# Chunk attention and ELU feed-forward: w_in operands kept by column tile, w_out's raw high quarters written later, out writes scheduled one by one

## The chip, the cores and the metric

The kernel runs on one core of a Trainium2 chip. The metric is the device time of one execution in microseconds (us), read as a median over runs. TensorE (PE) multiplies, VectorE (DVE), ScalarE (ACT) and GpSimd (POOL) work on tiles, and SyncE (SP) issues nearly all DMAs, in program order, from one queue.

## The reference

Eight heads of 576 tokens in 8 batches are attended in chunks of 64 tokens; the heads of a token are then laid side by side (4608 tokens of 512) and go through a feed-forward net with an ELU between its two products.

```python
scores = scale * np.matmul(q_c, k_c.transpose(0, 1, 2, 4, 3))   # 64 x 64 in each chunk
scores = scores - np.max(scores, axis=-1, keepdims=True)
attn = np.exp(scores)
attn = attn / (np.sum(attn, axis=-1, keepdims=True) + 1e-09)
out = np.matmul(attn, v_c)
...
h = x @ w_in                                                     # 4608 x 512 by 512 x 2048
g = np.where(h > 0.0, h, alpha * (np.exp(np.minimum(h, 0.0)) - 1.0))
return (g @ w_out).astype(np.float32)                            # by 2048 x 512
```

## The kernel before

**Precision.** Each operand of the feed-forward net is kept as a high part of fewer bits and a low part (names ending in `hi` and `lo`), and a product is three matmuls of 128x128 by 128x512 (`three`, line 431; its matmul is line 434). The weights arrive as 64-bit floats and are rebuilt from their halves in `prepare_units` and `merge_units`.

**Stages.** The 4608 tokens are 9 blocks of 512. Three are computed plainly: the first (with the loading of the weights among it), the second and the third (`FIRST_BLOCK`, `SECOND_BLOCK`/`LATER`, `THIRD_BLOCK`: strings in which each item is one step, emitted in that order). The other six are taken in three pairs, and each pair multiplies by a scheme of seven products of quarter matrices instead of eight, for w_in and again for w_out. The first pair is written out by hand (`PAIR`, and `KEPT` for its w_out products). The other two, called superblocks here, are ordered by a planner.

**Operands of the seven products.** For w_in they are made during the second block by `combine` (line 512): POOL adds and subtracts quarters (line 510), `write_parts` (line 534) writes the raw quarters from `wi_hi` and `wi_lo` to `a_dram` (line 537), `write_sums` (line 547) the four sums. For w_out, `Sums` makes four sums for each of eight pairs of row tiles j (`whole`, line 576; `sum`, line 591; `high`, 594; `low`, 597; `write_half`, 603) and writes them to `w_dram`; `write_raw` (line 652) writes raw quarters, two DMAs a call. In the superblocks the operands come back as entries of 512 KB into a ring of four slots (`load_entry`, line 1317). The low parts of w_out are also kept in `lo_dram` and loaded again into `wo_lo` (line 689).

**Attention.** While a block is multiplied, the attention of coming tokens runs beside it in tiles of 128 tokens: loads of q and k (line 227) and of v (line 206), turns by DVE (line 351), scores (line 248), softmax, a turn of the result by DVE (line 388), a copy by ACT (line 393), a swap of quarters between partitions by four small DMAs on SP's queue (`swap_turned`, line 399), and the product with v (`multiply_v`, line 256), which waits for that swap.

**Who sets the order.** The engines run their instructions in the order of the program. Up to `KEPT` that is the order of the strings; what `MORE_KEPT` and `RAW_SECOND` name is spread among their lines. In the superblocks the class `Plan` sets it: each job has a nominal time, estimated costs, what it reads and writes, and a due time followed back from the PE products that need it. A job of SP may hold several DMAs, and these are then issued as one. `add_sums` (line 1873) adds the w_out sums that are left (j of 2, 6 and 7, `LATE_SUMS`), `add_out` (line 1630) the writes of finished results: two turns by DVE (line 1637), then four DMAs (line 1645). `add_entry` adds the ring loads.

**Places.** The sums of j = 6 and 7 use room of the tiles `g_more`, in which the superblocks later keep hidden values (`g_place`); `g_more` lies in the places of `wo_hi` and `wo_lo` of the first half of w_out, and row 4 to 7 of it is named by `g`.

Of the kernel before, what the change touches and what calls it, by code (L numbers as in the profile page):

```python
# [10 lines left out]
F32 = mybir.dt.float32  # L11
F32R = mybir.dt.float32r
# [8 lines left out]
def kernel(  # L21
# [34 lines left out]
    Q = 32  # L56
# [32 lines left out]
    def w_in_tiles(pool):  # L89
        return [pool.tile([P, NK, NF // 2 * P], F32R, name=name) for name in ("wi_hi", "wi_lo")]  # L90
# [4 lines left out]
    def w_in_slices(f: int):  # L95
        half, f = divmod(f, NF // 2)
        return [w[:, :, f * P:(f + 1) * P] for w in weights[half][:2]]
# [414 lines left out]
    def combine():  # L512
# [18 lines left out]
        def rows(i: int, g: int, lo: int):  # L531
            return a_dram[i, g // 2, :, g % 2, lo].rearrange("p (k f) -> p k f", k=2)

        def write_parts(g, lo):
            w1, w2 = w_in_slices(2 * g)[lo], w_in_slices(2 * g + 1)[lo]
            for i, w in enumerate((w1[:, :2], w1[:, 2:], w2[:, 2:])):
                nc.sync.dma_start(out=rows(i, g, lo), in_=w.bitcast(F32))
# [454 lines left out]
    def dma(n: int, took: float):  # L992
        return 540 * n, 540 * (n - 1) + 2000 + took, took
# [24 lines left out]
    def warm(n: int):  # L1018
# [83 lines left out]
    RAW_SECOND = {3: (3, 1), 6: (4, 1), 9: (5, 1), 13: (3, 0), 14: (4, 0), 15: (5, 0)}  # L1102
# [11 lines left out]
        2: "w1a w1b", 3: "w1c", 4: "w1d", 5: "w1e w1f", 6: "w1g", 7: "w1h", 8: "w1i", 9: "w1j", 11: "R0", 13: "R1",  # L1114
        14: "R2", 15: "R3",
# [265 lines left out]
    def g_place(j: int, b: int):  # L1381
        if j < 4:
            return g_first[:, j, b]
        name = ("wo_hi", "wo_lo")[j // 2 - 2]
        return late_tile(name, lambda: w0.tile([P, 2, 4, TB], F32, name="g_more", tag=name))[:, j % 2, b]
# [46 lines left out]
    LATE_SUMS = (2, 0), (6, 6), (7, 18)  # L1432
# [197 lines left out]
    def add_out(t: float, s: int, h: int, c: int, sources, keys, place, place_keys):  # L1630
# [11 lines left out]
        def send():  # L1642
            for b in range(4):
                at = b * P + c * 2 * Q
                nc.sync.dma_start(
                    out=out[n0:n0 + TB, at:at + 2 * Q].rearrange("(t p) d -> p t d", p=Q),
                    in_=place()[b * Q:(b + 1) * Q].rearrange("p (t d) -> p t d", d=2 * Q))
# [3 lines left out]
        plan.add(t + .05, "SP", dma(4, 2300), send, list(place_keys), [])  # L1651
# [221 lines left out]
    def add_sums(t: float, j: int):  # L1873
        made, early = {}, j < NG // 2
        g = 2 if early else 4 + j % 2
# [9 lines left out]
        def whole(engine):  # L1885
# [6 lines left out]
            ("G", i, b) for i in ((4, 5) if early else (6, 7)) for b in range(4)]  # L1892
# [52 lines left out]
```

## Time and profile before

| what | value |
|---|---|
| median of 3 runs | 836.18 us (833.5 to 837.43) |
| the profiled execution | 833.86 us, of it 832.1 us span |
| mean granted PE clock | 0.992 |
| PE busy | 810.0 us (97%) |
| DVE, ACT, POOL busy | 616.4, 524.7, 171.5 us |
| moved by DMA | 191.90 MB, mean 231 GB/s |
| first, second, third block about | 27 to 130, 130 to 235, 235 to 325 us |
| hand-written pair, `KEPT`, superblocks about | 325 to 454, 454 to 505, 505 to 832 us |

In the profile a row of a group has the line, the engine, the operation and output<-inputs. `SPq` is SP issuing a DMA; the time beside it is that of the issue, not of the transfer. A row of a timeline has start, duration, engine, line, what, and in brackets how long the engine stood idle before it and what ended that. A row of a stretch has the stretch, its length, then the busy time of PE, PE's weight loads, DVE, ACT and POOL with instruction counts, the granted PE clock, the mean busy share of the 16 DMA engines, and GB/s.

### The profile page before, as it was taken

To read this page: it belongs to the slowest core of one execution; us is meant where nothing else is said; L and a number is where in the kernel's file an instruction comes from. 1 tells how busy PE (TensorE), PEld (TensorE's weight loads), DVE (VectorE), ACT (ScalarE), POOL (GpSimd) and SP (SyncE) were. 2 spreads that over 40 slices of the span, in tenths; PEclk is the share of its full clock that TensorE was granted. 3 is DMA by queue.
4 is the path that set the end of the run, shared out by engine and by line. 5 is a ranking of instruction groups with operands and counts; after the bars stand their busy time and mean duration, and the time that the engine had idled before them with its cause. 6 is when DMAs were issued, how large, how long until landed. Compare 5 with 4: busy or idle time off the path is not lost.

```text
span 832.1 us, 15856 instructions
## 1 busy us (share of the span) xinstructions
PE 810.0 (97%) x5853; PEld 659.8 (79%) x5853; DVE 616.4 (74%) x915; ACT 524.7 (63%) x990; POOL 171.5 (21%) x148
## 2 busy tenths in 40 slices
PE   7899999999989999999999999999999999999997
PEld 6688878888768878878888888877788878888886
DVE  4999997676856668767666867877799956557974
ACT  5999885444554545766666445988867736776551
POOL 0000014365425441434111263100020000000100
PEclk9999999999999999999999999999999999999999
DMA  9875984888879797679977787999865586555655
GB/s 259 249 223 192 298 289 132 246 258 243 251 222 248 208 264 213 215 242 268 291 228 193 213 235 247 317 272 274 253 203 205 189 245 204 187 194 201 212 194 152
DMA packets 189629, 191.90 MB, mean 231 GB/s; under 512 B 84976, under 2 KB 158192, under 8 KB 189552
## 3 DMA queue, kind: packets, MB, share of 16 engines
q1 hardware_dynamic: 188912, 188.80, 75.9%
q0 software_dynamic: 640, 2.10, 0.6%
q8 instruction: 46, 0.75, 0.4%
q14 instruction: 31, 0.25, 0.1%
HBM read 144.18 MB, written 42.99 MB: 225 GB/s over the span
## 4 chain that ended last, share of the span: by engine, by line
PE 78%; DMA 9%; DVE 4%; ACT 4%; SPq 3%; issue 1%; DVEq 0%; ACTq 0%
PE o L434 41%; PE h L434 32%; DMA ring<-a_dram 3%; PE ps_a L248 2%; PE ps_a L256 2%; DMA kept<-in_k_dram 1%; DMA turned<-unturned 1%; DMA kept<-in_q_dram 1%; SPq L227 1%; PE h L451 1%; SPq L206 1%; SPq L399 1%; PE ps_a L315 1%; DMA k_sb<-in_k_dram 1%; DMA wo_lo<-lo_dram 1%
## 5 line engine op out<-in xcount | busy, mean ns | idle before, releaser
L434 PE MATMUL o<-wo_hi,ghi 128*128 128x512 f32 x272 | 108.3, 398 | 0.0
L434 PE MATMUL o<-wo_hi,glo 128*128 128x512 f32 x272 | 107.0, 393 | 0.5 <-DVE glo L479 0.5
L434 PE MATMUL o<-wo_lo,ghi 128*128 128x512 f32 x272 | 106.6, 392 | 0.0
L434 PE MATMUL h<-xhi,wi_hi 128*128 128x512 f32 x228 | 83.9, 397 | 0.1
L434 PE MATMUL h<-xlo,wi_hi 128*128 128x512 f32 x228 | 82.3, 390 | 0.0
L434 PE MATMUL h<-xhi,wi_lo 128*128 128x512 f32 x180 | 70.2, 390 | 0.0
L434 PEld LDWEIGHTS o<-wo_hi,glo 128*128 128x128 f32 x272 | 51.3, 189 | 12.3 <-DVE glo L479 1.4
L434 PEld LDWEIGHTS o<-wo_hi,ghi 128*128 128x128 f32 x272 | 51.5, 189 | 11.3
L434 PEld LDWEIGHTS o<-wo_lo,ghi 128*128 128x128 f32 x272 | 51.5, 189 | 10.4
L510 POOL TENSOR_TENSOR kept<-wi_hi,wi_lo 128x512 f32<-128x512 f32 x16 | 22.2, 1405 | 157.9 <-DVE xf L172 117.8
L471 DVE SCALAR_TENSOR_TENSOR e<-e,h 128x512 f32<-128x512 f32 x48 | 32.8, 684 | 25.0 <-ACT e L469 24.7
L434 PE MATMUL o<-split,ring 128*128 128x512 f32 x216 | 51.0, 390 | 0.0
L434 PEld LDWEIGHTS h<-xhi,wi_hi 128*128 128x128 f32 x228 | 42.6, 188 | 9.8 <-ACT kept L785 0.8
L434 PEld LDWEIGHTS h<-xlo,wi_hi 128*128 128x128 f32 x228 | 42.8, 188 | 8.6
L434 PEld LDWEIGHTS o<-split,ring 128*128 128x128 f32 x216 | 40.5, 188 | 8.4
L393 ACT COPY unturned<-turned 128x512 f32<-128x512 f32 x28 | 17.4, 621 | 46.0 <-DVE turned L388 40.1
L468 ACT ACTIVATE e<-h 128x512 f32<-128x512 f32 x48 | 28.6, 597 | 27.5 <-PE h L434 21.9
L476 ACT CAST ghi<-e 128x512 fp32r<-128x512 f32 x48 | 29.8, 621 | 20.3 <-DVE e L471 20.2
L746 POOL TENSOR_TENSOR glo<-e,ghi 128x512 fp32r<-128x512 f32 x16 | 20.8, 1297 | 96.8 <-ACT ghi L744 96.8
L434 PE MATMUL h<-split,ring 128*128 128x512 f32 x168 | 40.4, 392 | 0.0
L1492 ACT ACTIVATE e<-e 128x512 f32<-128x512 f32 x64 | 39.5, 630 | 1.0
L434 PEld LDWEIGHTS h<-xhi,wi_lo 128*128 128x128 f32 x180 | 33.8, 188 | 7.2
(226 smaller groups left out, 2021.4 us busy)
## 6 DMA issues: line engine op xcount, KB each, us to landing
ring<-a_dram SPq DMA_DIRECT2D x56, 512.0 KB, 4.7
ring<-w_dram SPq DMA_DIRECT2D x56, 512.0 KB, 3.3
wi_hi<-a_dram SPq DMA_DIRECT2D x56, 256.0 KB, 5.1
kept<-in_q_dram SPq DMA_DIRECT2D x100, 128.0 KB, 3.4
kept<-in_k_dram SPq DMA_DIRECT2D x100, 128.0 KB, 4.0
wo_lo<-lo_dram SPq DMA_DIRECT2D x20, 512.0 KB, 5.7
v_sb<-in_v_dram SPq DMA_DIRECT2D x32, 256.0 KB, 5.6
st<-in_moe_w_in_dram SPq DMA_DIRECT2D x16, 512.0 KB, 4.2
```

What stands on the lines that cost most here:

```text
L206: nc.sync.dma_start(out=dst[p0:p0 + n], in_=src[b, :, s0:s0 + n, :].rearrange("h s d -> s h d"))
L227: nc.sync.dma_start(out=qk[p0:p0 + n // U, w0:w0 + NK * U * D].rearrange("p (h w) -> p h w", h=NK), in_=src[b, j::2, s0:s0 + n, :].rearran ...
L248: nc.tensor.matmul(scores[halves[c], j, hp, :], lhsT=qT[halves[j], hp, halves[c]], rhs=kT[halves[j], hp, halves[c]], start=True, stop=True,)
L256: nc.tensor.matmul(x_ps[halves[j], c, hp, :], lhsT=v_sb[halves[c], 2 * hp + j, :], rhs=aT[halves[c], :, j * NK + hp], start=True, stop=True,)
L393: nc.scalar.copy(out=unturned, in_=turned)
L434: nc.tensor.matmul(ps, lhsT=a, rhs=b, start=start, stop=stop, skip_group_check=onto)
L468: nc.scalar.activation(out=e, in_=h, func=AF.Relu, scale=-1.0)
L471: nc.vector.scalar_tensor_tensor(out=e, in0=e, scalar=-1.0, in1=h, op0=ALU.add, op1=ALU.max)
L476: nc.scalar.copy(out=ghi, in_=e)
L510: nc.gpsimd.tensor_tensor(out=out, in0=a, in1=b, op=op)
L746: engine.tensor_tensor(out=lo, in0=e, in1=hi.bitcast(F32), op=ALU.subtract)
L1492: nc.scalar.activation(out=units[u], in_=units[u], func=AF.Exp, scale=-1.0)
```

## The change

Four things change; what is computed stays.

1. `wi_hi` and `wi_lo` hold, for each tile of 128 columns, its four row tiles side by side (before: for each row tile all columns). A quarter that `write_parts` writes is then 1 KB in a row of SBUF instead of two runs of 512 B, and two of the three writes become one DMA: two DMAs a call instead of three.
2. The raw high quarters of the second half of w_out (`write_raw(3..5, 0)`, six DMAs of 256 KB) leave the second block (f = 13, 14, 15) for `KEPT` (f = 8, 10, 12).
3. The four DMAs of `add_out` become four jobs of the planner.
4. The sums of j = 6 and 7 have later nominal times (8 and 22 products after the start of the first superblock instead of 6 and 18) and rows 6 and 7 of `g_more` as their room instead of 4 and 5; rows 4 and 5 now lie where `wo_lo` was.

```diff
-        return [pool.tile([P, NK, NF // 2 * P], F32R, name=name) for name in ("wi_hi", "wi_lo")]
+        return [pool.tile([P, NF // 2, NK * P], F32R, name=name) for name in ("wi_hi", "wi_lo")]
...
-        return [w[:, :, f * P:(f + 1) * P] for w in weights[half][:2]]
+        return [w[:, f].rearrange("p (k f) -> p k f", k=NK) for w in weights[half][:2]]
...
-        def rows(i: int, g: int, lo: int):
-            return a_dram[i, g // 2, :, g % 2, lo].rearrange("p (k f) -> p k f", k=2)
-
         def write_parts(g, lo):
             w1, w2 = w_in_slices(2 * g)[lo], w_in_slices(2 * g + 1)[lo]
-            for i, w in enumerate((w1[:, :2], w1[:, 2:], w2[:, 2:])):
-                nc.sync.dma_start(out=rows(i, g, lo), in_=w.bitcast(F32))
+            nc.sync.dma_start(
+                out=a_dram[:2, g // 2, :, g % 2, lo, :].rearrange("i p w -> p i w"),
+                in_=w1.rearrange("p (i k) f -> p i (k f)", k=2).bitcast(F32))
+            nc.sync.dma_start(
+                out=a_dram[2, g // 2, :, g % 2, lo, :], in_=w2[:, 2:].rearrange("p k f -> p (k f)").bitcast(F32))
...
-    RAW_SECOND = {3: (3, 1), 6: (4, 1), 9: (5, 1), 13: (3, 0), 14: (4, 0), 15: (5, 0)}
+    RAW_SECOND = {3: (3, 1), 6: (4, 1), 9: (5, 1)}
...
-        2: "w1a w1b", 3: "w1c", 4: "w1d", 5: "w1e w1f", 6: "w1g", 7: "w1h", 8: "w1i", 9: "w1j", 11: "R0", 13: "R1",
-        14: "R2", 15: "R3",
+        2: "w1a w1b", 3: "w1c", 4: "w1d", 5: "w1e w1f", 6: "w1g", 7: "w1h", 8: "w1i W3", 9: "w1j", 10: "W4", 11: "R0",
+        12: "W5", 13: "R1", 14: "R2", 15: "R3",
...
-        name = ("wo_hi", "wo_lo")[j // 2 - 2]
+        name = ("wo_lo", "wo_hi")[j // 2 - 2]
...
-    LATE_SUMS = (2, 0), (6, 6), (7, 18)
+    LATE_SUMS = (2, 0), (6, 8), (7, 22)
...
-        def send():
-            for b in range(4):
-                at = b * P + c * 2 * Q
-                nc.sync.dma_start(
-                    out=out[n0:n0 + TB, at:at + 2 * Q].rearrange("(t p) d -> p t d", p=Q),
-                    in_=place()[b * Q:(b + 1) * Q].rearrange("p (t d) -> p t d", d=2 * Q))
+        def send(b: int):
+            at = b * P + c * 2 * Q
+            nc.sync.dma_start(
+                out=out[n0:n0 + TB, at:at + 2 * Q].rearrange("(t p) d -> p t d", p=Q),
+                in_=place()[b * Q:(b + 1) * Q].rearrange("p (t d) -> p t d", d=2 * Q))
...
-        plan.add(t + .05, "SP", dma(4, 2300), send, list(place_keys), [])
+        for b in range(4):
+            plan.add(t + .05 + .01 * b, "SP", dma(1, 575), lambda b=b: send(b), list(place_keys), [])
...
-        g = 2 if early else 4 + j % 2
+        g = 2 if early else 6 + j % 2
...
-            ("G", i, b) for i in ((4, 5) if early else (6, 7)) for b in range(4)]
+            ("G", i, b) for i in ((6, 7) if early else (4, 5)) for b in range(4)]
```

PE's order of products stays as it was; the tables of the change move SP's DMAs above all. Three places of SP's queue follow. A row is line, DMA, output<-input, shape, and how many in a row.

The end of the second block and the start of the third, before: the writes of w_in's quarters (`a_dram<-wi_..`), of sums (`a_dram<-kept`) and of w_out's raw high quarters (`w_dram<-wo_hi`) stand ahead of a swap of the attention (`turned<-unturned`).

```order
L537 DMA a_dram<-wi_lo 128x2x128 x3
L652 DMA w_dram<-wo_hi 256x1x256 x2
L547 DMA a_dram<-kept 128x4x256 x2
L537 DMA a_dram<-wi_hi 128x2x128 x3
L652 DMA w_dram<-wo_hi 256x1x256 x2
L537 DMA a_dram<-wi_lo 128x2x128 x3
L227 DMA kept<-in_q_dram 16x4x256 x8
L227 DMA kept<-in_k_dram 16x4x256 x8
L652 DMA w_dram<-wo_hi 256x1x256 x2
L547 DMA a_dram<-kept 128x4x256 x2
L537 DMA a_dram<-wi_hi 128x2x128 x3
L399 DMA turned<-unturned 32x256 x4
```

The same place in the change, from the second half of the first write on:

```order
L536 DMA a_dram<-wi_lo 128x256
L547 DMA a_dram<-kept 128x4x256 x2
L533 DMA a_dram<-wi_hi 128x2x256
L536 DMA a_dram<-wi_hi 128x256
L533 DMA a_dram<-wi_lo 128x2x256
L536 DMA a_dram<-wi_lo 128x256
L227 DMA kept<-in_q_dram 16x4x256 x8
L227 DMA kept<-in_k_dram 16x4x256 x8
L547 DMA a_dram<-kept 128x4x256 x2
L533 DMA a_dram<-wi_hi 128x2x256
L536 DMA a_dram<-wi_hi 128x256
L399 DMA turned<-unturned 32x256 x4
```

Ten DMAs fewer stand between the swap before this one and the swap shown: four of w_in's writes, six raw quarters. What follows the swap (loads of q, k and v, writes of the first block's results, the next swap) stays in its order.

The end of `KEPT`, before: sums of j = 1 (`w_dram<-g_kept`), loads for the attention, the first four ring entries, and the low parts of j = 2 (`g_kept<-lo_dram`).

```order
L603 DMA w_dram<-g_kept 128x2x256 x2
L689 DMA wo_lo<-lo_dram 128x1024
L227 DMA kept<-in_q_dram 32x4x256 x4
L227 DMA kept<-in_k_dram 32x4x256 x4
L1317 DMA ring<-a_dram 128x1024 x4
L584 DMA g_kept<-lo_dram 128x1024
```

The same place in the change:

```order
L603 DMA w_dram<-g_kept 128x2x256
L652 DMA w_dram<-wo_hi 256x1x256 x2
L603 DMA w_dram<-g_kept 128x2x256
L689 DMA wo_lo<-lo_dram 128x1024
L227 DMA kept<-in_q_dram 32x4x256 x4
L227 DMA kept<-in_k_dram 32x4x256 x4
L652 DMA w_dram<-wo_hi 256x1x256 x2
L1317 DMA ring<-a_dram 128x1024
L652 DMA w_dram<-wo_hi 256x1x256 x2
L1317 DMA ring<-a_dram 128x1024 x3
L584 DMA g_kept<-lo_dram 128x1024
```

The six raw quarters now stand ahead of the ring's entries 2 to 4 and of the low parts, four of them ahead of the first entry too.

The start of the last superblock, before: ring entries and out writes.

```order
L1317 DMA ring<-a_dram 128x1024 x2
L1645 DMA out_dram<-g_kept 32x16x64 x8
L1317 DMA ring<-a_dram 128x1024 x2
L1645 DMA out_dram<-g_kept 32x16x64 x4
L1317 DMA ring<-a_dram 128x1024 x24
```

In the change:

```order
L1317 DMA ring<-a_dram 128x1024 x2
L1644 DMA out_dram<-g_kept 32x16x64 x5
L1317 DMA ring<-a_dram 128x1024
L1644 DMA out_dram<-g_kept 32x16x64 x3
L1317 DMA ring<-a_dram 128x1024
L1644 DMA out_dram<-g_kept 32x16x64
L1317 DMA ring<-a_dram 128x1024
L1644 DMA out_dram<-g_kept 32x16x64 x3
L1317 DMA ring<-a_dram 128x1024 x23
```

The third ring entry has three out writes fewer ahead of it, the fifth three fewer; the fourth as many as before. In the first superblock the eight writes of the sums of j = 6 and 7 stand later among the ring loads (before, three of the eight stood ahead of the superblock's first swap, now none), three loads of q earlier, and of the work on these sums one addition moves from POOL to DVE and two subtractions from DVE to POOL.

## The prediction

> **What bounds the kernel now.** I read the page's busy times first, then the list of waits for PE alone, then the stretches in which PE is not full.
>
> ```profile
> PE 810.0 (97%) x5853; PEld 659.8 (79%) x5853; DVE 616.4 (74%) x915; ACT 524.7 (63%) x990; POOL 171.5 (21%) x148
> PE ps_a L256 <- DMA turned<-unturned: 2.9, 3, 2.4
> PE h L434 <- DMA ring<-a_dram: 1.8, 2, 1.3
> PE o L434 <- DMA ring<-a_dram: 1.3, 4, 0.7
> ```
>
> PE is the bound: 22 us of 832.1 are not busy, and PE's program stays as it is. The change can only give or take idle time of PE, and what a pause does to PE's clock. The waits say where: one of 2.4 us for a swap of the attention, and six for ring entries, 3.1 us together. The stretches around them (length, then PE, PE's loads, DVE, ACT, POOL; clock, DMA share and GB/s last):
>
> ```profile
> 244.00:250.00 6.00, 3.35 (x71) 2.48 (x70) 1.42 (x2) 1.81 (x3) 4.53 (x3) 0.94 0.72 201
> 248.00:254.00 6.00, 5.82 (x46) 4.73 (x47) 4.17 (x8) 1.73 (x3) 2.25 (x3) 0.72 0.74 214
> 540.00:544.00 4.00, 3.65 (x17) 2.69 (x16) 2.49 (x5) 3.84 (x12) 0.00 (x0) 1.00 1.05 361
> 560.00:572.00 12.00, 10.40 (x44) 7.68 (x43) 9.17 (x15) 9.32 (x17) 0.00 (x0) 1.00 1.01 271
> 584.00:592.00 8.00, 7.10 (x29) 5.15 (x29) 6.88 (x12) 7.73 (x15) 0.00 (x0) 1.00 0.95 250
> 676.00:686.00 10.00, 8.23 (x35) 6.24 (x35) 4.06 (x6) 5.70 (x10) 0.00 (x0) 1.00 1.03 293
> ```
>
> Row one: PE idles 6.00 - 3.35 = 2.65 us. Row two: behind that pause the clock is granted at 0.72 of full speed for 6 us, which costs (1 - 0.72) x 6 = 1.7 us more. No other pause after the first block costs clock: the rows from 540 on have 1.00. So there are three pools of time: **4.3 us** at the swap, 0.35 + 1.60 + 0.90 = **2.85 us** in the first superblock, and **1.77 us** at the start of the last one.
>
> **Quarters of w_in and w_out, second block.** The swap that PE waits for, with what SP issues ahead of it (SP's rows of the timeline, then ACT's copy that feeds the swap, and PE):
>
> ```profile
> 204.90 2.48 SPq L399 DMA_DIRECT2D turned<-unturned  x4
> ...
> 208.04 1.69 SPq L537 DMA_DIRECT2D a_dram<-wi_lo  x3
> 209.78 1.26 SPq L652 DMA_DIRECT2D w_dram<-wo_hi  x2
> ...
> 212.40 2.57 SPq L537 DMA_DIRECT2D a_dram<-wi_hi  x3
> 215.00 1.19 SPq L652 DMA_DIRECT2D w_dram<-wo_hi  x2
> 216.24 1.73 SPq L537 DMA_DIRECT2D a_dram<-wi_lo  x3
> ...
> 226.10 1.19 SPq L652 DMA_DIRECT2D w_dram<-wo_hi  x2
> ...
> 228.62 2.93 SPq L537 DMA_DIRECT2D a_dram<-wi_hi  x3
> ...
> 239.59 0.62 ACT L393 COPY unturned<-turned 128x512 f32<-128x512 f32 x1 [2.70 <-DVE turned L388]
> 243.68 3.12 SPq L399 DMA_DIRECT2D turned<-unturned  x4
> 247.65 0.30 PE L256 MATMUL ps_a<-turned,v_sb 64*64 64x64 f32 x2 [2.42 <-DMA turned<-unturned]
> ```
>
> From 204.90 SP issues without a pause: each row begins where the one ahead ends. ACT has the data ready at 239.59 + 0.62 = 240.21, SP comes to the swap at 243.68, 3.5 us late, and PE has stood since 247.65 - 2.42 = 245.23. The change takes out of that queue one of three issues at four places, (1.69 + 2.57 + 1.73 + 2.93) / 3 = 2.97 us, and six raw quarters, 1.26 + 1.19 + 1.19 = 3.64 us: 6.6 us. SP would be at the swap by 243.68 - 6.6 = 237.1, so the copy becomes the last to come, at 240.21. From issue to PE's start it took 247.65 - 243.68 = 3.97 us, with all its traffic beside it; the same again ends at 244.2, 1.0 us ahead of need. The stall goes with its clock: **-4.3 us**. Bounds: 0 if the transfer turns out to be what is late, -4.3 if all goes. I take the upper one, for the margins are 3.1 us on SP's queue and 1.0 us behind it. What is late next there: nothing by more than the other two waits of that row, 2.9 - 2.4 = 0.5 us, which I leave.
>
> A rule bears on the second half of this term. The row: 2.65 us of idleness, then 0.72 of the clock. The Trainium skill (TensorE: Matmul & The Clock Gate, "HAM oscillation — how this bites in real kernels") wants no pause of PE above about 3.4 us; read so, this pause would leave the clock alone, and the term would be 2.65 and not 4.3 us. The trace disagrees, and the sum goes by the trace.
>
> The layout of w_in itself: matmuls, casts and subtractions have the same number and size of elements, and PE, ACT and DVE keep their instructions. I cost it at nothing: what a cast or a subtraction gained or lost would lie beside a PE that is busy 97% of the span.
>
> **Raw quarters in KEPT.** The six DMAs come back at about 484 to 494 us, 6 x 256 KB = 1.57 MB.
>
> ```profile
> L652 SPq DMA_DIRECT2D w_dram<-wo_hi x6: 525/598/640, 209.8 to 226.7; - x6
> 484.00:500.00 16.00, 16.00 (x72) 13.25 (x71) 11.33 (x9) 6.32 (x9) 8.75 (x5) 1.00 0.98 276
> 500.00:516.00 16.00, 16.00 (x131) 13.09 (x130) 11.59 (x18) 7.85 (x15) 5.51 (x5) 1.00 0.71 216
> g_kept<-lo_dram SPq DMA_DIRECT2D x1, 512.0 KB, 9.5
> 494.08 0.32 SPq L584 DMA_DIRECT2D g_kept<-lo_dram  x1
> 505.68 1.28 DVE L576 TENSOR_TENSOR g_kept<-wo_hi,g_kept 128x512 f32<-128x512 f32 x2
> 509.20 0.69 DVE L1471 TENSOR_TENSOR g_kept<-o,kept 128x512 f32<-128x512 f32 x1 [0.64 <-issue]
> L434 PE MATMUL o<-wo_lo,ring x72: 388/389/501, 514.2 to 581.1; 128*128 128x512 f32 x72
> ```
>
> On SP's queue they are 6 x 0.6 = 3.6 us; as transfers, at the 250 GB/s between these two rows, 1.57 MB / 250 GB/s = 6.3 us. The DMA engines are full (0.98) until 500, then have (1 - 0.71) x 16 = 4.6 us free: most of the work drains there. The last to feel it is the load of low parts: issued at 494.08, landed 9.5 us later, 503.6; now 3.6 to 6.3 us later, 507.2 to 509.9. DVE wants it at 505.68 (L576) and stands 1.5 to 4.2 us in its order; behind it waits L1471, at 509.20, which frees the bank that PE writes again at 514.2 (the first matmul of `o<-wo_lo,ring`). L1471 ended at 509.89, so 4.3 us cover the delay. I take **0**, with 0 to +6.3 as bounds: nothing if the pause of 500 to 516 takes it in, all of it if the ring loads behind have to wait one for one.
>
> **Sums of j = 6 and 7.** Their work keeps its amount; the change puts their eight writes later among the ring loads and three loads of q earlier. Up to 560 us the DMA total differs by the quarters above alone, and behind that SP's queue is in the old order, so the waits of 560 to 592 stay. DVE gains one addition (0.68 us, half of L576's 1.28) and loses two subtractions. POOL now does six in a row:
>
> ```profile
> 509.13 0.74 POOL L591 TENSOR_TENSOR g_more<-g_more 128x256 f32<-128x256 f32 x1
> 511.62 1.18 POOL L591 TENSOR_TENSOR g_more<-g_more 128x256 f32<-128x256 f32 x1
> ```
>
> 4.4 to 7.1 us, and SP's writes of these sums wait for it with ring loads behind them. Bounds for both together: -2.85 us (all three waits gone) to +2.7 (what the six take on POOL above 4.4, paid by PE). I take **0**.
>
> **Out writes.** The start of the last superblock on SP:
>
> ```profile
> 664.23 3.04 SPq L1317 DMA_DIRECT2D ring<-a_dram  x2
> 669.84 4.39 SPq L1645 DMA_DIRECT2D out_dram<-g_kept  x8
> 674.33 0.96 SPq L1317 DMA_DIRECT2D ring<-a_dram  x2
> 675.39 2.30 SPq L1645 DMA_DIRECT2D out_dram<-g_kept  x4
> 677.78 10.82 SPq L1317 DMA_DIRECT2D ring<-a_dram  x5
> ```
>
> An out write takes 4.39 / 8 = 0.55 us of the queue. The third ring entry, behind five of them, goes at 669.84 + 2.75 = 672.6 instead of 674.33, 1.7 us sooner, more than the longest ring wait of the list above (1.3 us). The fourth stays. The fifth, behind nine writes and two entries (0.48 us each), goes at about 675.8 instead of 677.78. So the pauses shrink by 1.7 us at most; the transfers still share engines that are full (1.03), and I take **-1.3 us**, between 0 and -1.77.
>
> **Sum.** -4.3 + 0 + 0 - 1.3 = -5.6 us on the profiled execution's 833.86: 828.3 us, span 826.5. The profiled execution lies 2.3 us under the median of the three runs, 836.18. Carried over to it, 836.18 - 5.6 = **830.6 us**.
>
> **Rivals.**
> *The swap stays late.* If not the queue but the transfer is slow (3.97 us from issue to PE's start), PE stands again, and a pause just as long brings the clock down again. Then only the out writes count: 836.18 - 1.3 = 834.9. For it: v loads and out writes of the first block stand ahead of the swap in both orders. Against it: SP has 3.1 us to spare.
> *Half a gain.* The swap is on time, but the first superblock pays for later sums and a fuller DMA: its 2.85 us of pauses double to 5.7. 836.18 - 5.6 + 2.85 = 833.4. For it: DMA shares of 1.01 to 1.05 there. Against: the free 4.6 us ahead.
> *Slower: the raw quarters are paid in full.* Place: the ring entries from 500 us on. If the free engine time behind 500 is not used because SP issues later loads sooner, all 6.3 us end on the ring, and one of the pauses is long enough to bring the clock down as at 248 us: 6.3 + 1.7 = 8.0 against 5.6 gained, 838.6 us. It decides from 5.6 us on, when 5.6 / 6.3, nine tenths of the added transfer, are unhidden.
> *No effect at all*, both waits merely moving to the next transfer, is 836.2.
>
> **Chances.** Forecast 0.57; half a gain 0.19; swap stays late 0.10, no effect 0.05; slower 0.09. A measurement of this kernel can tell about 0.5% from no change, 4.2 us: faster is below 832.0, slower above 840.4. The forecast lies 1.4 us under that line; nearly all of it is counted as faster, with a little of the half gain, 0.58. The slower rival as priced lies within 0.5%, and only with a second fall of the clock above: slower 0.07, the rest 0.35. Range: below, the forecast with the first superblock's waits going too, 830.6 - 2.85 - 0.5 = 827.2, and 0.7 for the spread of runs, 826.5; above, past the swap that stays late, to no effect, 836.5. The forecast's own range is 827 to 832.
>
> **What would show it.** Right: PE's wait for `turned<-unturned` falls from 2.9 to under 1 us and the clock is 1.00 in every stretch from 240 to 260 us; SP issues the swap within 1 us of the end of ACT's copy; PE idles under 0.7 us at the start of the last superblock; the low parts of j = 2 land at 507 to 510 us less the 4.3 us that all has moved up, without a PE wait before 540. Wrong: a PE pause of 2 us or more anywhere in 490 to 600 with a clock under 1.00 behind it; ring waits above 5 us in the first superblock; SP standing at a write of `g_more` for POOL; or the old pause in the third block with the copy long done.

## The result: 825.42 us, ratio 0.989

The changed kernel has a median of 825.42 us (825.15 to 827.57, 4 runs) against 834.84 us (833.38 to 837.43, 4 runs) of the kernel before: a ratio of 0.9889, 95% interval [0.9856, 0.9923], or -9.3 us [-12.0, -6.4]. The forecast was 830.6 us, -5.6; the first result lies 1.1 us below the range. Measured a second time (run e9 below) the ratio was 0.9915 [0.9883, 0.9947], -7.1 us [-9.8, -4.4], and the median of 828.55 us lies inside the range. The direction stands in both. The gain is larger than forecast by 3.7 us in the first and by 1.5 us in the second, whose interval holds the forecast's -5.6 too. Ratios and intervals, here and below, are the recorded ones and not exactly the quotients of the medians beside them.

The profile after: the page's busy times and PE's waits for the swaps and for the ring.

```profile
span 823.4 us, 15851 instructions
PE 804.4 (98%) x5853; PEld 655.6 (80%) x5853; DVE 613.1 (74%) x914; ACT 523.5 (64%) x990; POOL 171.1 (21%) x149
PE ps_a L256 <- DMA turned<-unturned: 0.3, 1, 0.3
PE o L434 <- DMA ring<-a_dram: 1.3, 3, 0.6
```

PE has the same 5853 matmuls and is busy 804.4 instead of 810.0 us. Of these 5.6 us 2.65 lie in the second block (94.64 to 91.99 between the points used below), where a fall of the clock is gone: part of the gain is clock, not idle time. Another 2.45 lie ahead of it (216.52 to 214.07), where PE's idle time grew by almost as much, so they are no gain. The wait for the swap fell from 2.9 to 0.3 us, and the ring's wait that stood with `h` (1.8 us) is gone from the list.

The stretches of the changed kernel that answer to those of the prediction (length, then PE, PE's loads, DVE, ACT, POOL; clock, DMA share, GB/s), and behind them, in a fence of its own, one of the kernel before:

```profile
234.00:260.00 26.00, 26.00 (x261) 21.02 (x260) 15.88 (x24) 12.60 (x21) 11.68 (x10) 1.00 0.82 221
516.00:546.00 30.00, 28.71 (x182) 22.41 (x181) 24.79 (x41) 26.97 (x63) 1.30 (x1) 1.00 0.95 291
546.00:572.00 26.00, 26.00 (x233) 21.24 (x232) 18.96 (x31) 20.87 (x49) 0.00 (x0) 1.00 1.04 309
572.00:600.00 28.00, 27.78 (x180) 22.26 (x179) 21.93 (x35) 24.81 (x69) 1.30 (x1) 1.00 0.84 251
676.00:686.00 10.00, 10.00 (x45) 8.27 (x45) 7.17 (x11) 7.95 (x14) 0.00 (x0) 1.00 0.70 247
```

```profile
234.00:260.00 26.00, 23.33 (x180) 18.60 (x179) 15.01 (x22) 10.44 (x17) 9.75 (x9) 0.93 0.77 212
```

The second block has no pause left (26.00 of 26.00, before 23.33) and the clock is 1.00 (before 0.93). The start of the last superblock has none either (10.00 of 10.00; the changed kernel is some 7 us further on there, but in its whole stage from 596.2 to 727.5 PE is busy throughout). The first superblock still has 1.29 + 0.22 us of pauses.

To see where the time went I take five points of PE's program that both kernels have: the last start of five kinds of matmul (the first start for `o<-split,ring`). Before:

```profile
L451 PE MATMUL h<-xlo,wi_hi x12: 389/389/397, 31.0 to 225.8; 128*128 128x512 f32 x12
L434 PE MATMUL h<-xhi,wi_lo x180: 388/389/398, 33.2 to 323.4; 128*128 128x512 f32 x180
L434 PE MATMUL o<-wo_hi,glo x272: 387/389/632, 36.8 to 504.6; 128*128 128x512 f32 x136
L434 PE MATMUL o<-split,ring x216: 388/389/501, 603.4 to 824.5; 128*128 128x512 f32 x108
L434 PE MATMUL o<-wi_lo,ring x144: 388/389/501, 507.6 to 736.8; 128*128 128x512 f32 x144
```

The same rows of the changed kernel:

```profile
L451 PE MATMUL h<-xlo,wi_hi x12: 389/389/393, 30.8 to 225.6; 128*128 128x512 f32 x12
L434 PE MATMUL h<-xhi,wi_lo x180: 388/389/504, 33.1 to 317.9; 128*128 128x512 f32 x180
L434 PE MATMUL o<-wo_hi,glo x272: 388/389/499, 36.6 to 499.2; 128*128 128x512 f32 x136
L434 PE MATMUL o<-split,ring x216: 388/389/501, 596.2 to 815.9; 128*128 128x512 f32 x108
L434 PE MATMUL o<-wi_lo,ring x144: 387/389/501, 502.2 to 727.5; 128*128 128x512 f32 x144
```

The differences between neighbours are the stages: 225.8 to 323.4 holds the late swap, 323.4 to 504.6 the pair and `KEPT`, 504.6 to 603.4 the first superblock's beginning, 603.4 to 736.8 the start of the last superblock.

| stage | before | after | change | forecast |
|---|---|---|---|---|
| up to the first point | 225.8 | 225.6 | -0.2 | 0 |
| second block, late swap | 97.6 | 92.3 | -5.3 | -4.3 |
| pair and `KEPT` | 181.2 | 181.3 | +0.1 | 0 |
| first superblock | 98.8 | 97.0 | -1.8 | 0 |
| start of the last superblock | 133.4 | 131.3 | -2.1 | -1.3 |
| the rest | 95.3 | 95.9 | +0.6 | 0 |
| span | 832.1 | 823.4 | -8.7 | -5.6 |

Three stages gave more than forecast. The queue at the swap, of the changed kernel (SP, then ACT's copies and PE, which are other engines):

```profile
227.37 0.62 ACT L393 COPY unturned<-turned 128x512 f32<-128x512 f32 x1 [2.97 <-DVE turned L388]
228.01 2.41 SPq L399 DMA_DIRECT2D turned<-unturned  x4
...
235.89 2.85 SPq L486 DMA_DIRECT2D out_dram<-io  x4
238.84 0.41 SPq L206 DMA_DIRECT2D v_sb<-in_v_dram  x1
239.02 0.62 ACT L393 COPY unturned<-turned 128x512 f32<-128x512 f32 x1 [2.70 <-DVE turned L388]
239.66 2.47 SPq L399 DMA_DIRECT2D turned<-unturned  x4
...
244.44 0.65 PE L256 MATMUL ps_a<-turned,v_sb 64*64 64x64 f32 x32
```

SP issues the swap at 239.66, 0.02 us after ACT's copy ends at 239.64; before it was 3.5 us. PE starts at 244.44 with no wait shown.

### The profile page after: what moved, and what is told of

Read it like the earlier page. It is cut to its first block, busy times and chain, and to the rows that moved or that the text cites. A ratio compares the mean times of both kernels' runs of the same rounds, so it can differ in the third digit from the quotient of the medians.

```text
span 823.4 us, 15851 instructions
## 1 busy us (share of the span) xinstructions
PE 804.4 (98%) x5853; PEld 655.6 (80%) x5853; DVE 613.1 (74%) x914; ACT 523.5 (64%) x990; POOL 171.1 (21%) x149
## 4 chain that ended last, share of the span: by engine, by line
PE 83%; DMA 8%; SPq 3%; ACT 2%; DVE 2%; issue 1%; DVEq 0%; ACTq 0%
PE o L434 43%; PE h L434 34%; DMA ring<-a_dram 3%; PE ps_a L248 2%; PE ps_a L256 2%; SPq L206 2%; PE h L451 1%; DMA st<-in_moe_w_out_dram 1%; DMA kept<-in_k_dram 1%; DMA a_dram<-wi_lo 1%; DMA kept<-in_q_dram 1%; DMA a_dram<-wi_hi 1%; DMA v_sb<-in_v_dram 1%; PE ps_a L315 1%; DMA ring<-w_dram 1%
```

## The experiments

The four parts, named for this section: **layout** (w_in by column tile, merged writes), **raw** (w_out's raw high quarters in `KEPT`), **outs** (out writes one by one), **sums** (j = 6 and 7 later, rooms exchanged). All stages below are the same differences as in the table above, read from each run's profile.

| run | parts | second block | pair, `KEPT` | first superbl. | last superbl. start | median us | ratio to before |
|---|---|---|---|---|---|---|---|
| before | none | 97.6 | 181.2 | 98.8 | 133.4 | 834.84 | 1 |
| changed | all | 92.3 | 181.3 | 97.0 | 131.3 | 825.42 | 0.9889 [0.9856, 0.9923] |
| e1 | layout | 93.7 | 181.2 | 98.5 | 133.0 | 830.88 | 0.9965 [0.9944, 0.9987] |
| e2 | raw | 92.6 | 181.2 | 98.2 | 135.0 | 828.25 | 0.9927 [0.99, 0.9953] |
| e3 | all, 12 writes added | 101.3 | 181.2 | 97.8 | 132.5 | 836.18 | 1.0026 [1.0006, 1.0046] |
| e4 | none, raw on ACT's queue | 105.1 | 181.3 | 97.6 | 135.0 | 841.36 | 1.0081 [1.0054, 1.0108] |
| e5 | all but outs | 92.0 | 181.5 | 99.1 | 132.8 | 827.95 | 0.9898 [0.987, 0.9925] |
| e6 | all but sums | 92.5 | 181.2 | 101.0 | 131.4 | 827.7 | 0.9891 [0.986, 0.9923] |
| e7 | outs | 98.4 | 181.3 | 102.4 | 131.6 | 832.83 | 0.9959 [0.9937, 0.9982] |
| e8 | sums | 99.5 | 181.3 | 97.5 | 135.2 | 835.84 | 0.9999 [0.9977, 1.0021] |
| e9 | all, again | 94.0 | 181.2 | 99.1 | 131.4 | 828.55 | 0.9915 [0.9883, 0.9947] |
| e10 | layout, raw | 92.6 | 181.2 | 97.3 | 133.5 | 829.27 | 0.9926 [0.9903, 0.995] |
| e11 | all but layout | 93.8 | 181.2 | 97.9 | 131.6 | 827.39 | 0.9916 [0.9889, 0.9943] |
| e12 | all but raw | 94.5 | 181.2 | 100.0 | 131.7 | 830.09 | 0.9948 [0.9928, 0.9969] |

Runs e1 to e4 shared one chip and its runs of the kernel before (median 833.48 us), e5 to e8 another (835.85), e9 to e12 a third (836.02).

### e1: the layout alone

```diff
-        return [pool.tile([P, NK, NF // 2 * P], F32R, name=name) for name in ("wi_hi", "wi_lo")]
+        return [pool.tile([P, NF // 2, NK * P], F32R, name=name) for name in ("wi_hi", "wi_lo")]
 ...
-            for i, w in enumerate((w1[:, :2], w1[:, 2:], w2[:, 2:])):
-                nc.sync.dma_start(out=rows(i, g, lo), in_=w.bitcast(F32))
+            nc.sync.dma_start(
+                out=a_dram[:2, g // 2, :, g % 2, lo, :].rearrange("i p w -> p i w"),
+                in_=w1.rearrange("p (i k) f -> p i (k f)", k=2).bitcast(F32))
 ...
```

> The kernel before with the new layout of w_in and its two writes a call instead of three; the rest as before. Theory A, SP's queue: the swap was late because SP had too many issues ahead of it. This edit takes out four of them between the two swaps at 205 and 232 us (3.0 us by the rows of before), so SP reaches the swap of 243.7 us at about 240.7, within 0.5 us of ACT's copy; the pause of 2.65 us and the half clock behind it go, -4 to -5 us, ratio 0.994 to 0.995. Theory B, the transfers: the bytes are the same, so the pause stays, 0 to -0.5 us. Theory C, the two edits add up: about half of the gain, -2 to -2.5 us.

Measured 830.88 us, 0.9965 [0.9944, 0.9987]. SP's issue of the swap, ACT's copy and PE, then the stretch:

```profile
239.14 0.62 ACT L393 COPY unturned<-turned 128x512 f32<-128x512 f32 x1 [2.70 <-DMA kept<-in_k_dram]
241.63 2.90 SPq L399 DMA_DIRECT2D turned<-unturned  x4
245.70 1.12 PE L256 MATMUL ps_a<-turned,v_sb 64*64 64x64 f32 x32 [0.96 <-DMA turned<-unturned]
```

```profile
234.00:260.00 26.00, 24.90 (x254) 19.96 (x254) 15.00 (x22) 12.14 (x20) 10.14 (x9) 1.00 0.86 228
```

The swap is still 241.63 - 239.76 = 1.9 us late, PE stands 1.1 us in place of 2.67, and the clock stays at 1.00. So 1.6 us of idle time less, and the whole of the clock's share. The merged writes free less of the queue than the forecast's 2.97 us: at the four places SP issues for 1.05 + 2.42 + 1.12 + 2.32 = 6.9 us instead of 8.9, 2.0 us less; the merged DMA itself takes 0.58 to 1.27 us to issue. In program time the layout alone is worth -2.9 us [-4.7, -1.1]; that alone does not choose between theory A (-4 to -5) and theory C (-2 to -2.5).

### e2: the raw quarters alone

```diff
-    RAW_SECOND = {3: (3, 1), 6: (4, 1), 9: (5, 1), 13: (3, 0), 14: (4, 0), 15: (5, 0)}
+    RAW_SECOND = {3: (3, 1), 6: (4, 1), 9: (5, 1)}
 ...
-        2: "w1a w1b", 3: "w1c", 4: "w1d", 5: "w1e w1f", 6: "w1g", 7: "w1h", 8: "w1i", 9: "w1j", 11: "R0", 13: "R1",
-        14: "R2", 15: "R3",
+        2: "w1a w1b", 3: "w1c", 4: "w1d", 5: "w1e w1f", 6: "w1g", 7: "w1h", 8: "w1i W3", 9: "w1j", 10: "W4", 11: "R0",
+        12: "W5", 13: "R1", 14: "R2", 15: "R3",
```

> The kernel before with the six raw high quarters written in the later stage; the rest as before. Theory A: 3.6 us leave SP's queue, the swap goes at about 240.3 us, the pause and its clock go: -4 to -5 us, as much as with the layout alone, so that the two do not add up. Theory B: 1.57 MB of transfers leave the place, the pause goes too, -4 to -5. Theory C: -2 to -2.5. In all of them the low parts of j = 2 land 3 to 6 us later and DVE waits for them 1 to 4 us without a wait of PE before 540 us.

Measured 828.25 us, 0.9927 [0.99, 0.9953]. The second block takes 92.6 us, as with all four parts.

```profile
237.63 0.62 ACT L393 COPY unturned<-turned 128x512 f32<-128x512 f32 x1 [2.70 <-DVE turned L388]
238.28 2.46 SPq L399 DMA_DIRECT2D turned<-unturned  x4
```

The swap goes as soon as the copy is done (238.25). The two parts do not add up: layout alone takes 3.9 us from the stage (97.6 to 93.7), raw alone 5.0, both 5.0 (e10). That is what a queue says, whose lateness can be removed only once. In program time it is -2.9 us for the layout, -6.1 [-8.3, -3.9] for the raw quarters and -6.2 [-8.1, -4.2] for both, too wide to decide it alone. DVE waits 1.63 us for the low parts of j = 2, as expected (1 to 4).

### e3: the changed kernel with twelve small writes put into SP's queue

```diff
             write_raw(*RAW_SECOND[f])
+        if f > 12:
+            for d in range(12 // 3):
+                nc.sync.dma_start(
+                    out=w_dram[f - 9, 2 + d % 2, :16, :, 0, :HALF],
+                    in_=weights[1][2][:16, 4 * (d % 2):4 * (d % 2) + 4:2, :HALF].bitcast(F32))
```

> The changed kernel with twelve more writes of 32 KB each in the second block, four each at f = 13, 14 and 15, where the raw quarters stood before (they write rows that are written again later). They load SP's queue by 12 x 0.5 = 6 us, but move only 0.4 MB, a quarter of the six raw quarters. Theory A: of the 6 us some 2 are taken by SP's pause at 226 us and at 239 us, the swap goes some 4 us late, PE stands 2 to 3 us at the product with v, the clock falls behind it: +4 to +5 us over the changed kernel. Theory B: the transfers stay light, no pause, 0 to +0.5 us.

Measured 836.18 us, 1.0026 [1.0006, 1.0046] of the kernel before, so 1.1 to 1.4% above the changed one (by its two ratios).

```profile
228.41 0.62 ACT L393 COPY unturned<-turned 128x512 f32<-128x512 f32 x1 [4.07 <-DVE turned L388]
229.87 3.22 SPq L1288 DMA_DIRECT2D w_dram<-wo_hi  x4
236.79 2.52 SPq L399 DMA_DIRECT2D turned<-unturned  x4
240.36 1.47 PE L256 MATMUL ps_a<-turned,v_sb 64*64 64x64 f32 x32 [3.62 <-DMA turned<-unturned]
```

```profile
208.00:234.00 26.00, 24.60 (x193) 19.22 (x192) 20.40 (x27) 14.45 (x26) 8.83 (x7) 1.00 0.53 152
234.00:260.00 26.00, 22.38 (x172) 17.89 (x172) 15.14 (x22) 9.71 (x17) 7.75 (x7) 0.87 0.79 225
```

These writes carry little: the DMA engines are at 0.53 and 152 GB/s ahead of the late swap. Yet the swap goes 236.79 - 229.03 = 7.8 us after its copy, and PE stands 3.62 us. A late queue is enough to bring the pause back, without the traffic. The rival that the transfer is slow loses its ground: from the swap's issue to PE's start it takes 3.57 us here, less than the 3.97 of before, and the pause is longer.

The price is larger than expected: the second block takes 9.0 us more than in the changed kernel (101.3 against 92.3), not 4 to 5. It is not the number of DMAs alone. The twelve writes hold SP for 3.92 + 5.10 + 3.22 = 12.2 us, and in each group of four the last two write the same rows as the first two: SP stands 1.4 + 2.6 + 0.8 = 4.8 us until those have landed. The issues are the other 7.4 us, 0.6 each. So the run sets the queue against the traffic, not the count of DMAs against SP's waits.

### e4: the raw quarters of f = 13 to 15 on ACT's queue

```diff
-    def write_raw(n: int, lo: int):
+    def write_raw(n: int, lo: int, queue=nc.sync):
 ...
-            nc.sync.dma_start(
+            queue.dma_start(
 ...
-            write_raw(*RAW_SECOND[f])
+            write_raw(*RAW_SECOND[f], nc.scalar if f > 12 else nc.sync)
```

> The kernel before with the six raw high quarters in their old place, but issued by ACT on its own queue instead of SP. Same bytes at the same time, 3.6 us less on SP's queue. Theory A: as with the raw quarters moved, pause gone, -4 to -5 us (less what six issues on ACT cost, under 1 us if ACT needs as long as SP, 0.6 us each, at places where ACT is half busy). Theory B: the bytes are still there, the pause stays, 0 to -0.5 us.

Measured 841.36 us, 1.0081 [1.0054, 1.0108], slower, which neither theory expected. SP's own waits, and its timeline:

```profile
SPq L537 <- DMA w_dram<-wo_hi: 11.6, 1, 11.6
```

```profile
200.28 13.02 SPq L537 DMA_DIRECT2D a_dram<-wi_hi  x3
```

SP stood 11.6 us at one of its writes for a transfer that ACT was to issue, and did issue at 209.95: the program counts the DMAs of both queues with the same semaphores, in turn, so that a DMA on SP waits for one that ACT issues late. The run made a new wait in place of the old one and does not tell queue and traffic apart; e3 does.

### e5: all but the single out writes

```diff
-        for b in range(4):
-            plan.add(t + .05 + .01 * b, "SP", dma(1, 575), lambda b=b: send(b), list(place_keys), [])
+        plan.add(t + .05, "SP", dma(4, 2300), send, list(place_keys), [])
```

> The changed kernel with the out writes in fours again; all else is as changed. As forecast (the out writes are worth the pause of PE at the start of the last superblock and nothing else): that start loses 1.3 us, at most 1.8, the clock stays at 1.00 there, and the time is 825.4 + 1.3 = 826.7 us. Theory that the pause also brings the clock down in a part of the executions (the kernel with the raw quarters alone had 2.0 us of pause there and the clock at 0.92 to 0.94, 1.8 us more): a pause of 1.7 to 2.1 us comes back, the median rises by 2 to 4 us, to 827.4 to 829.4, and the executions spread over several us again, as those of the kernel before do (830.8 to 838.4). No effect: 825.4, and a ring wait at that place that is as short as now.

Measured 827.95 us (827.41 to 829.24), 0.9898 [0.987, 0.9925]. The start of the last superblock takes 132.8 us, 1.5 more than with the out writes single, and the pause is back, though smaller than expected, with the clock at 1.00:

```profile
660.00:676.00 16.00, 14.91 (x67) 12.02 (x66) 9.11 (x15) 4.74 (x9) 0.29 (x1) 1.00 0.82 236
```

The program's time does not resolve these 1.5 us: the ratio of 0.9898 lies between the two of the changed kernel (0.9889 and 0.9915), and the executions do not spread over several us, as one of the theories had it.

### e6: all but the sums

```diff
-    LATE_SUMS = (2, 0), (6, 8), (7, 22)
+    LATE_SUMS = (2, 0), (6, 6), (7, 18)
 ...
-        g = 2 if early else 6 + j % 2
+        g = 2 if early else 4 + j % 2
 ...
```

> The changed kernel with the sums of j = 6 and 7 at their old times (and the two rooms in their old order). As forecast (sums worth 0): 825.4 us, and pauses of PE in the first superblock as now, about 1.5 us together. Theory that the sums bring 1.3 to 1.7 us: the pauses of the first superblock go back to 2.3 to 2.9 us, that superblock takes 1.0 to 1.7 us longer, and the time is 826.7 to 827.1 us.

Measured 827.7 us (826.29 to 829.43), 0.9891 [0.986, 0.9923]. The first superblock took 101.0 us in the profiled execution, 4.0 more than in the first profile of the changed kernel, beyond the 1.0 to 1.7 that the theory of the sums has. But e9 shows the changed kernel itself with 99.1, so this single figure decides nothing, and the ratio is nearly that of the changed kernel's first measurement (0.9889).

### e7: the single out writes alone

```diff
-        plan.add(t + .05, "SP", dma(4, 2300), send, list(place_keys), [])
+        for b in range(4):
+            plan.add(t + .05 + .01 * b, "SP", dma(1, 575), lambda b=b: send(b), list(place_keys), [])
```

> The kernel before with the out writes one by one, nothing else. As forecast: 1.3 us less than the kernel before, 832.2 us by its median of 833.5, PE idle under 0.7 us at the start of the last superblock. Theory of pause and clock: 2 to 4 us less, 829.5 to 831.5, and less spread. The swap's wait of 2.4 us in the second block and the clock of about 0.72 behind it stay in either case. No effect: 833.5.

Measured 832.83 us against 835.85, 0.9959 [0.9937, 0.9982]: -3.4 us [-5.3, -1.5]. No pause at the start of the last superblock, and the swap's pause as in the kernel before, but dearer:

```profile
676.00:686.00 10.00, 10.00 (x45) 7.96 (x43) 4.81 (x8) 4.30 (x8) 0.00 (x0) 1.00 0.97 255
...
234.00:260.00 26.00, 21.98 (x174) 17.53 (x173) 14.24 (x23) 10.77 (x18) 8.21 (x8) 0.93 0.75 208
```

Made alone, the out writes are worth more than 1.3 us by this interval. The profiled execution was the longest of the twelve (837.47 us), so its swap's pause may be dearer than a usual one. The executions still spread (830.1 to 837.47), so the spread does not come from the start of the last superblock alone.

### e8: the sums alone

```diff
-    LATE_SUMS = (2, 0), (6, 6), (7, 18)
+    LATE_SUMS = (2, 0), (6, 8), (7, 22)
 ...
```

> The kernel before with the sums of j = 6 and 7 later and the rooms exchanged, nothing else. As forecast: 833.5 us, no change. Theory that the sums bring 1.3 to 1.7 us: pauses of PE in the first superblock of 1.5 us or less in place of 2.85, 831.8 to 832.2 us. The swap's wait and its clock stay in either case.

Measured 835.84 us against 835.85, 0.9999 [0.9977, 1.0021]: no change, as forecast. The start of the last superblock shows the pause with a fall of the clock, which the first profile of the kernel before did not have:

```profile
680.00:684.00 4.00, 1.75 (x8) 1.15 (x7) 2.08 (x3) 1.89 (x3) 0.00 (x0) 0.97 0.85 247
684.00:688.00 4.00, 4.00 (x13) 3.15 (x12) 0.60 (x1) 1.62 (x3) 0.00 (x0) 0.60 1.04 270
```

A pause of 2.25 us, and behind it 4 us at 0.60, another 1.6 us. This profiled execution, too, was the longest of its twelve (839.15 us).

### e9: the changed kernel again

No edit.

> The changed kernel as it is, beside the three below on one chip. Theory that the gain is larger than forecast because the executions of the kernel before spread with the length of the swap's pause (its two medians so far are 833.5 and 835.9, a stage of 97.6 to 99.5 us from the last of the first block's h<-xlo,wi_hi to the last h<-xhi,wi_lo, against 92.0 to 92.6 without the pause): a ratio of 0.987 to 0.991, a spread of the changed kernel's executions of half that of the kernel before or less, and again 92.0 to 92.8 us in that stage. If the first result was a lucky draw instead: a ratio above 0.992 and executions up to 830 us.

Measured 828.55 us (824.71 to 830.03, 6 runs) against 836.02, 0.9915 [0.9883, 0.9947]. The ratio lies just outside the expected 0.987 to 0.991, and the rest did not hold either: the second block took 94.0 us, not 92.0 to 92.8, and its six executions spread over 5.3 us, more than half of the 8.7 us of the kernel before's 22. The first four runs were a good draw as well.

### e10: layout and raw quarters without the two others

The edits of e5 and e6 together, both undone.

> The change without the out writes and without the sums (layout and raw quarters only). As forecast, the two others together are worth 1.3 us: 1.3 us above the changed kernel. By the stages of the traces so far, out writes 2.5 (131.5 against 134.1 us) and sums 0.5 to 1.5: 3 to 4 us above the changed kernel, 828.5 to 829.5 where that has 825.4. If both only look so by the spread of single profiles: equal within 0.7 us.

Measured 829.27 us (824.85 to 833.61, 12 runs), 0.7 us above e9, inside the spread of both. That is not the 3 to 4 us expected from the stages; the forecast's 1.3 us and no difference cannot be told apart here. The start of the last superblock, 133.5 us, again is 2.1 above e9's 131.4; the first superblock, 97.3, is 1.8 below e9's 99.1.

### e11 and e12: all but the layout, all but the raw quarters

The edits of e1 and of e2, undone in the changed kernel.

> The change without the layout of w_in and its merged writes (raw quarters, out writes, sums stay). Theory of SP's queue: the raw quarters alone free 3.6 us of it and the swap was 3.5 us late, so the pause stays gone and the time is that of the changed kernel within 0.7 us. If the layout does something of its own (copies and subtractions of a tile of w_in are faster or slower, or transfers lighter): 1 us or more apart.

> The change with w_out's raw high quarters in the second block as before (layout, out writes, sums stay). Theory of SP's queue: 3.0 us of it freed, the swap still 0.5 to 2 us late, a pause of PE of 0.5 to 1.5 us that leaves the clock alone: 0.7 to 2 us above the changed kernel. If the raw quarters in KEPT cost something of their own: at or below the changed kernel's time.

Without the layout 827.39 us (e9: 828.55): 1.2 us less, where within 0.7 was expected, but the intervals of the two ratios overlap almost wholly. Nothing is seen to be lost, and no worth of the layout beside the raw quarters is shown. Without the raw quarters 830.09 us (e9: 828.55), 1.5 more, as expected, though these intervals overlap as well. There the swap goes at 243.43, 3.0 us after its copy, and PE stands over 2 us, both more than expected, with the clock untouched:

```profile
247.47 1.12 PE L256 MATMUL ps_a<-turned,v_sb 64*64 64x64 f32 x32 [2.03 <-DMA turned<-unturned]
```

```profile
242.00:246.00 4.00, 3.44 (x45) 2.56 (x43) 3.39 (x3) 2.69 (x4) 2.19 (x2) 1.00 1.05 325
246.00:250.00 4.00, 2.39 (x38) 2.00 (x39) 0.88 (x3) 0.70 (x2) 2.52 (x2) 1.00 0.64 180
250.00:254.00 4.00, 4.00 (x19) 3.29 (x18) 3.74 (x8) 1.15 (x2) 1.99 (x3) 1.00 0.87 233
```

## Why the prediction was right in direction and too small

**What failed.** The mechanism of the two terms that count, SP's queue ahead of the swap and the out writes ahead of the ring entries, held; their sizes did not. On the profiled executions the swap's -4.3 measured -5.3 and the out writes' -1.3 measured -2.1; the first superblock, put at 0, measured -1.8, and how much of that is the change stays open. The 2.3 us added to come to the median measured 0.3.

**Second block: right mechanism, term too small.** The queue was what held the swap, shown by e3 (a late queue with light traffic brings the pause back) and by e2 with e10 (two parts that do not add up). SP's issue within 1 us of the copy, the clock of 1.00 and the wait under 1 us came as listed. The term of -4.3 measured -5.3 in the two first profiles. There PE's idle time in the stage fell from 2.96 to 0.31 us, the -2.65 of the forecast, and its busy time from 94.64 to 91.99, again 2.65. Of the latter 1.7 is the clock, as forecast; the other 0.95 is busy time at full clock, for which no cause is shown. It is not much more than profiles differ by: the nine without a fall of the clock in this stage are busy there for 91.8 to 92.8 us, the kernel before, less the 1.7, for 92.9.

Over all profiles, three with the old queue (before, e7, e8) take 97.6 to 99.5 us, mean 98.5, and seven with the raw quarters moved on their own queue (changed, e2, e5, e6, e9, e10, e11) 92.0 to 94.0, mean 92.8: -5.7 us. The reason stands in the stretch from 234 to 260: idle time plus clock lost is 2.67 + 0.07 x 26 = 4.5 us before, 4.02 + 0.07 x 26 = 5.8 in e7 and 3.01 + 0.13 x 26 = 6.4 in e8. So for the median the step that failed is that I took the pause and its clock from one execution, the mildest of the three. How far it was too mild is less sure: the profiles of e7 and e8 are of the longest of their twelve executions, and in program time e2 and e10 have -6.1 and -6.2 us with intervals that both reach to -4.3.

The margin was misjudged too: I had SP 3.1 us ahead of the copy, but the swap before it also became one that waits for ACT (228.01, right at the end of its copy), and SP came with 239.66 - 239.25 = 0.4 us to spare (239.25 is where its v load ends).

**Raw quarters in `KEPT`: right, 0.** The stage from 323 to 504 us took 181.2 to 181.5 us in all fourteen profiles, with the six DMAs in it and without. The first superblock, where the bound of +6.3 would have been paid, takes 97.0 to 101.0 us in the eight profiles with them (mean 98.4) and 97.5 to 102.4 in the six without (mean 99.1). The low parts of j = 2 and DVE's wait for them, in the changed kernel:

```profile
493.14 0.38 SPq L584 DMA_DIRECT2D g_kept<-lo_dram  x1
...
501.59 1.29 DVE L576 TENSOR_TENSOR g_kept<-wo_hi,g_kept 128x512 f32<-128x512 f32 x2 [1.26 <-DMA g_kept<-lo_dram]
```

DVE's addition starts when they have landed, at 501.6, sooner than the 502.9 to 505.6 that follow from the prediction's 507.2 to 509.9 less 4.3. The landing moved up by 2.0 us (from 503.6) and PE's program at that place by 5.4 (504.6 to 499.2), so against the program it came 3.4 us later, just under the 3.6 to 6.3 that I priced. DVE stood 1.26 us, and PE did not wait for it. One sign did not come as listed: PE waits for ring entries before 540, at 520.26, 536.16 and 539.73, 0.31 + 0.39 + 0.56 us, where the kernel before has its first at 561.64. Whether the quarters or the later sums moved these waits is not shown; all pauses of the stage together fell from 2.85 to 1.5 us. The rival in which the quarters are paid in full, and are slower, is out.

**Sums of j = 6 and 7: 0, not refuted.** The first pair shows -1.8 us in the first superblock, and I took that for a miss. Over all profiles the seven with the sums later take 97.0 to 100.0 us, mean 98.3, the seven without 97.3 to 102.4, mean 99.1: -0.8 us, less than each group's own spread. e8 measured 0.9999 [0.9977, 1.0021]. So the bound of +2.7 is out, a gain of up to about 2 us is not, and how much of the first pair's -1.8 is the change stays open.

**Out writes: right mechanism, term too small.** SP's queue in the changed kernel, from the first out write on:

```profile
662.66 2.63 SPq L1644 DMA_DIRECT2D out_dram<-g_kept  x5
665.39 0.50 SPq L1317 DMA_DIRECT2D ring<-a_dram  x1
...
668.92 1.17 SPq L1317 DMA_DIRECT2D ring<-a_dram  x1
```

The third ring entry goes 665.39 - 662.66 = 2.73 us after the first out write and the fifth 6.26, where the forecast has 2.75 and 6.0 and the kernel before 4.49 and 7.94. I took -1.3 of a pause of 1.77, because "the transfers still share engines that are full". That discount is the step that failed: the whole pause goes. With single out writes the stage takes 131.3 to 132.5 us in seven profiles (mean 131.6), without 132.8 to 135.2 in seven (mean 134.0): -2.4 us. This is beyond my bound of -1.77, because in some executions the pause is longer and takes the clock with it, as in e2, e4 and e8; the profile of before had 1.00 there. This is read from the stages. In program time the out writes alone gain 3.4 us (e7), and beside the other parts their worth is not resolved (e5, e10).

**Carrying over to the median: the base was a draw.** I added 2.3 us, the distance of the profiled execution to the median of three. The changed kernel's profiled execution lay 0.3 us under its median in the first result and 1.5 us above it in e9 (830.03 against 828.55). It is no constant of the kernel. That and the terms make up the miss: 3.1 us on the profiled execution (828.3 forecast, 825.15 measured), 2.1 us by the offset.

**The sum by measured terms** is -5.7 + 0 - 0.8 - 2.4 = -8.9 us, between the -9.3 and -7.1 of the two comparisons, with the -0.8 open and the -5.7 leaning on two long executions.

**The rivals.** A swap that stays late and no effect are refuted by the second block's stage (92.3 and 94.0 us against 97.6). Half a gain asked for 5.7 us of pauses in the first superblock; the changed kernel has 1.5 there, and 2.7 in e9.

## What to carry to other kernels

A pause should be priced from several executions, or with a bound for the dearer case: one profile may show the mildest, and so may the place that looks cheap because its pause happened to leave the clock alone. Where one queue is late, two cuts that each suffice are worth one of them, so price the queue's lateness and not the sum of the cuts; and count the time that the queue is held, by issues and by waits, not bytes. For effects under some 2 us, the length of a stage between two matmuls that all variants have, over several variants, tells more than the time of the whole program.

## What the runs showed of the hardware that was not expected

**What counts for the clock is PE's idle time in one step of 3.41 us, not the length of the pause.** In all fourteen traces the granted clock is either 1.00 or 0.50, and between 45 and 810 us it stays at 0.50 for 3.41 or 6.83 us at a time, which costs 1.7 or 3.4 us. Within a trace the falls start whole multiples of 3.41 us apart (kernel before: 13.79, 27.44 and 249.31, which is 4 and 69 steps), so the steps do not start with the pause. Pauses of PE, the most idle time that falls into one such step, and how long the clock was at 0.50 from the next step on:

| where | pause, us | most in one step, us | clock at 0.50, us |
|---|---|---|---|
| e1, swap | 0.96 and 0.14 | 1.10 | 0 |
| before, start of last superblock | 1.33 (0.44 more 6 us later) | 1.33 | 0 |
| e12, swap | 2.03 | 1.20 | 0 |
| e1, start of last superblock | 1.67 | 1.67 | 0 |
| e7, first superblock | 1.78 | 1.73 | 0 |
| e4, next swap | 1.51 and 0.31 | 1.82 | 3.41 |
| e2, start of last superblock | 2.03 | 1.90 | 3.41 |
| e8, swap | 2.50 | 1.90 | 6.83 |
| before, swap | 2.42 and 0.24 | 1.99 | 3.41 |
| e4, start of last superblock | 2.01 | 2.01 | 3.41 |
| e8, start of last superblock | 2.25 | 2.25 | 3.41 |
| e3, swap | 3.62 | 2.42 | 6.83 |
| e7, swap | 2.70 and 0.15 | 2.85 | 3.41 |
| e4, swap | 6.35 | 3.41 | 6.83 |

From 45 to 810 us every step with 1.82 us or more of idle time was followed by a fall, and none with 1.73 or less, as far as the clock was at 1.00 in it. Two pauses of the same 2.03 us differ by where they lie: in e2 1.90 of it are in one step, in e12 it is split between two. A pause of some 2 us therefore costs its own length or nearly twice that, by chance. The Trainium skill (TensorE: Matmul & The Clock Gate, "HAM oscillation — how this bites in real kernels") has about 3.4 us for this; these traces have it earlier.

**One kernel's executions differ in places that no part of the change touches.** The first point of PE's program is reached between 224.2 and 228.6 us in the fourteen profiles, in no order of the parts. Two causes are seen but not separated: the first 36 us, in which PE is busy 24.4 to 27.6 us with a clock of 0.91 to 1.00, and short waits for loads. The spread of a single execution is thus about as large as the effects of two of the four parts.

**DMAs of two queues can hold each other up** (e4): where the program counts them with the same semaphores in turn, one issued on ACT's queue late made SP stand for 11.6 us.
